# Eight more weight slices decoded by halves, two more chunks of the attention turned on VectorE, and a reordered first part of the step list

## The chip, the cores and the metric

The kernel runs on one core of a Trainium2 chip. The metric is the device time of one execution in microseconds (us); lower is better. Engines are called PE (TensorE, with PEld for its weight loads), DVE (VectorE), ACT (ScalarE), POOL (GpSimd) and SP (SyncE, which issues the transfers here).

## The reference

A gated linear attention layer feeds a two-layer block with a hard-swish.

```python
# q, k, v, alpha: (4, 8, 768, 48) float32
for t in range(S):
    state = alpha[:, :, t, :, None] * state + einsum('bhd,bhe->bhde', k[:, :, t], v[:, :, t])
    y[:, :, t] = einsum('bhd,bhde->bhe', q[:, :, t], state)
x = y.transpose(0, 2, 1, 3).reshape(3072, 384)
h = x @ w_in                       # (384, 2048), float64 as it comes in
g = h * clip(h + 3, 0, 6) / 6
out = g @ w_out                    # (2048, 384), float64 as it comes in
```

## The kernel before

**Chunks and groups.** The 3072 tokens are 24 chunks of 128, six to each of the four batches. Two chunks make a group for the two dense layers. Groups 0 and 1 run the first layer with plain matmuls (`ff1` at L493, `ff1_half` at L504); group 0 also runs the second layer so (`ff2`, L531). From then on both layers run by schemes with fewer products: the first layer in 20 products per group (`product1`, L617), the second in seven (`product`, L720).

**The step list.** Nothing is looped or scheduled by the compiler. One string of 1798 words, run by `run` under `manual_schedule`, gives the program order of every engine. A word is a step and its arguments: `la.1` loads alpha of chunk 1, `f.1.7.0` is `ff1` of group 1, pair of columns 7, into PSUM bank m0. Each engine takes its own instructions from this list strictly in order, and waits where an input is not there or a buffer is not free.

**Steps of the attention, by chunk j:** `la lk lq lv` (loads, SP), `ta tk tq` (turning alpha, k, q so that head dimensions lie on partitions), `ca` (alpha to its place), `r` and `p` (scans, L321 and L333, DVE), `k` and `q` (scaled k and q, DVE), `sc` (scores, PE L360), `m` (masked scores, DVE L370), `kb` and `ck` (k by token, PE L388 and ACT L392), `u` (state update, PE L444), `sm` (next state, DVE L454), `st` (POOL L423), `sv` and `qa` (state and q laid beside the values and scores, ACT L433 and L380), `ya` and `yb` (the two halves of the output, PE L470), `cy` (output kept as the dense layer's input, ACT L479).

**Two ways to turn a chunk.** For a chunk below `FIRST` a load is one transfer of 192 KB in rows of 192 B into `rings`; `ta`, `tk`, `tq` are four PE transposes each (L283) into a PSUM bank, and `ca` is an ACT copy (L312). From `FIRST` on a load is four transfers in rows of 640 and 768 B (352 KB in all, each row once for two bands of partitions) into `quads`, with two small POOL memsets (L259) the first time that each of the two buffers is used; `tk` and `tq` are DVE transposes by 32x32 blocks in pairs (`turned`, L291), `ca` is the DVE transpose `by_blocks` (L287), `k` and `q` read SBUF instead of PSUM (L343), and `q` is followed by a small POOL memset (L347).

**Weights.** They come as float64. The kernel loads 16 slices (`w.0` to `w.7` of `w_in`, `w.8` to `w.15` of `w_out`, 768 KB each) into five raw buffers (`HOMES` says which) and turns each into float32:

- `d1` (`round_low`, ACT L185) rounds the low word, `d2` (`magnitude`, ACT L195) takes the high word without its sign.
- `d3` (`high_bits`, DVE): for a slice in `BY_HALVES` two instructions (L202 and L204), for the others three (L206, L207 and L209; the third puts the sign back).
- `dx` (`sign`, ACT L190), only for a slice in `BY_HALVES`: one instruction that writes the sign into the upper half of the low word.
- `d4` (`add_low`, POOL L216) adds the two words and frees the raw buffer.

`w_in`'s slice i serves column pair i of the first layer (`fa.i`, `fb.i`, `f.g.i`), and two slices of `w_out` serve a quarter of `ff2` (`b.c.part`).

**Around the dense layers.** `fr` (ACT L509) and `fg` (DVE L513) gate a bank of `ff1` and so free it; there are four such banks. `x` and `y` (DVE L664 and L554 to L558) prepare the weight sums of the later schemes, `s`, `xc` and `o` (DVE) the other sums. `z.m.n` (`idle`, L548) multiplies the identity n times into bank m: filler that keeps PE running. Until step 424 there are 46 such blocks.

Of the kernel before, what the change touches and what calls it, by code (L numbers as in the profile page):

```python
# [17 lines left out]
def kernel(  # L18
# [153 lines left out]

    BY_HALVES = {0, 1, 2, 4}

    def slice_of(i):
# [2 lines left out]
        return dst, lo, hi  # L180
# [31 lines left out]
    def add_low(i):  # L212

        dst, lo, hi = slice_of(i)
        high = dst if i in BY_HALVES else hi
        nc.gpsimd.tensor_tensor(out=dst.bitcast(I32), in0=high.bitcast(I32),  # L216
# [59 lines left out]
    def transposed(name, j, i=None):  # L276
        if j >= FIRST:
            turned(name, name, j)
            return
        t = bank("t" + name, j, i)  # L280
        src = ring[name, j % NR]
        for p in range(NP):
            nc.tensor.transpose(  # L283
                t[:, p], src[:, 2 * p : 2 * p + 2].rearrange("s h d -> s (h d)"), ident)
# [5 lines left out]
    def turned(to, name, j):  # L290
        nc.vector.transpose(  # L291
            out=turns[to].rearrange("r w p (u b) -> r p w b u", b=V // 2),
            in_=quads[name, j % NQ].rearrange("r p (w b) d -> r p w b d", w=2)[..., 0:BLK])
# [42 lines left out]
    def scaled(name, j):  # L336

        t = (K_t if name == "k" else Q_t)[j] = (Ks if name == "k" else Qs)[j % 2]
        by = R_t[j][:, :, 1:W] if name == "k" else without_first(P_t.pop(j))
        if j < FIRST:  # L340
            nc.vector.tensor_tensor(out=t, in0=ps_t.pop(("t" + name, j)), in1=by, op=ALU.mult)
# [428 lines left out]

    with tc.manual_schedule():
        run("""la.1 z.0.2 z.0.5 ta.1.2 la.0 ca.1 lq.1 z.0.2 ta.0.3 z.0.2 w.0 r.1 p.1 tq.1.2 z.0.2
               la.2 z.0.2 ca.0 r.0 z.0.2 lk.0 z.0.8 q.1 d1.0 p.0 lq.0 dx.0 ta.2.0 z.0.2 lv.0.0 d2.0
               tk.0.1 z.0.2 k.0 lk.1 w.1 tq.0.2 ca.2 kb.0.1 z.0.2 w.2 q.0 ck.0 r.2 qa.0.1 lq.2
               sc.0.0.2 z.0.2 z.0.2 la.3 qa.1.0 z.0.3 qa.1.1 m.0 p.2 lk.2 u.0.1.3 tk.1.0 lv.1.1
               z.0.2 w.3 d2.1 d1.1 sm.0.0 k.1 sv.0.1 dx.1 la.4 kb.1.1 z.0.1 ck.1 sm.0.1 sv.0.0
               tq.2.3 d3.0 d1.2 sc.1.2.1 d4.0 d3.1 lk.3 st.1 z.0.3 dx.2 q.2 m.1 d2.2 z.0.2 tk.2.3
               ta.3.0 k.2 ca.3 d3.2 u.1.2.1 sv.1.0 r.3 lq.3 sm.1.0 sm.1.1 ya.0.3 yb.0 cy.0 ta.4.0
               d4.1 fa.0.1 sv.1.1 ca.4 fa.1.2 sc.2.2.1 p.3 d2.3 d4.2 d3.3 ya.1.0 yb.1 w.5 d1.3 m.2
               fa.2.0 tk.3.3 lv.3.0 d4.3 k.3 w.6 cy.1 lk.4 st.2 fb.2 kb.2.2 kb.3.1 r.4 lv.2.2 d2.5  # L780
               d1.5 fr.0.2.0 fb.1 ck.2 tq.3.0 qa.2.0 d3.5 tk.4.3 d1.6 k.4 q.3 f.0.3.3 ck.3 sv.2.0
               d2.6 sc.3.2.1 u.2.0.1 u.3.2.3 qa.3.1 fr.0.3.1 d4.5 w.7 fg.0.2 lq.4 d3.6 f.0.5.0
               sm.2.0 d2.7 w.8 fg.0.3 d1.7 sv.2.1 kb.4.0 d4.6 ck.4 sm.2.1 st.3 d2.8 la.5 d3.7 sv.3.0
               qa.3.0 sm.3.0 w.9 f.0.6.3 qa.2.1 lk.5 d4.7 sv.3.1 tq.4.0 fb.0 m.3 sm.3.1 fr.0.1.0
               ta.5.1 p.4 fg.0.1 d3.8 w.4 fr.0.5.1 ca.5 fg.0.5 fr.0.0.0 d1.8 ya.2.2 yb.2 w.10 d4.8
               cy.2 fg.0.0 lq.5 ya.3.3 yb.3 cy.3 d2.9 la.6 f.0.7.2 lv.4.1 d1.9 d3.9 f.1.7.0 d4.9 r.5
               fr.0.7.0 d1.4 fr.0.6.1 dx.4 d1.10 w.12 q.4 fg.0.7 p.5 fg.0.6 d2.4 f.1.1.1 d2.10 d3.4
               tq.5.2 fr.1.7.1 tk.5.1 fr.1.1.0 la.7 f.1.0.2 d2.12 k.5 f.1.3.3 lv.5.0 ca.6 w.11 d4.4
               fg.1.7 lk.6 fg.1.1 fr.1.3.1 d3.10 d1.12 q.5 f.1.6.0 fr.1.0.0 fg.1.3 fg.1.0 qa.0.0
               d3.12 d4.10 lk.7 qa.5.0 ca.7 f.1.2.1 d2.11 kb.5.3 st.4 fr.1.6.1 tk.6 ck.5 f.1.4.2  # L790
               w.13 qa.4.0 fg.1.6 d1.11 sc.5.1.0 sc.4.3.2 u.4.3.0 u.5.1 d4.12 fa.4.3 d3.11 d4.11 m.4
               fr.1.4.1 fr.1.2.0 f.1.5.0 fb.4 w.15 lq.6 sm.4.0 fg.1.2 b.0.0.1 fg.1.4 d2.13 d1.13
               sv.4.1 r.6 d3.13 w.14 fr.0.4.0 b.1.0.2 k.6 sm.4.1 d2.15 sv.4.0 fg.0.4 tq.6 b.0.1
               fr.1.5.1 d1.15 b.1.1 d3.15 p.6 d4.13 st.5 fg.1.5 qa.4.1 tk.7 d2.14 s.1.1.1 s.1.0.0
               d1.14 d3.14 d4.15 qa.5.1 m.5 kb.6.3 b.0.2 d4.14 P.1.0.0 sm.5.0 s.1.3.2 s.1.2.3
               P.1.1.3 y.1 q.6 lk.8 x.0 x.1 K.1.0 lk.9 y.5 y.0 y.3 sv.5.0 x.2 sv.5.1 b.0.3 s.1.5
               ck.6 b.1.2 y.2 y.6 r.7 b.1.3 lv.6.2 y.9 G.1.0.0 P.1.2 k.7 K.1.1 y.8 y.10 y.7 y.11
               la.8 s.1.4 y.4 ya.4.1 yb.4 bo.1 cy.4 xc.2.0 ya.5.0 yb.5 cy.5 xc.2.1 y.16 sc.6.3.2
               u.6.1.2 P.1.3.3 K.1.2 xc.2.3 y.12 P.1.4 xc.2.4 y.15 x.3 so.1 lv.7.0 G.1.1.1 y.13
               P.1.5 bo.0 y.17 xc.2.5 y.19 P.1.6 xc.2.7 G.1.2.2 y.20 xc.2.6 y.18 O.1.2 y.21 M.2.0.2  # L800
               y.23 M.2.15.3 n.2.0.8 xc.2.2 M.2.1 xc.2.8 n.2.1.9 la.9 M.2.16 ca.8 sm.6.0 sv.6.1
               G.1.3.3 xc.2.9 sm.6.1 tk.8 p.7 m.6 r.8 la.10 kb.7.1 M.2.2 M.2.7.0 y.14 lq.7 n.2.2.10
               M.2.3 M.2.4 lq.8 n.2.7.11 M.2.8 n.2.4.12 p.8 ck.7 z.1.3 st.7 o.2.0.0 M.2.18.1 e.2.0.0
               xc.2.10 M.2.9 sv.7.0 tq.7 O.1.3 h.2.0 o.2.1.0 M.2.5 q.7 e.2.1.1 k.8 h.2.1 tk.9 M.2.10
               kt.8 n.2.10.14 u.7.0.2 y.22 n.2.5.13 sc.7.1.2 n.2.18.10 qa.6.1 M.2.11 n.2.11.15
# [149 lines left out]
```

## Time and profile before

| | |
|---|---|
| time, median of 3 runs | 531.0 us (530.9 to 531.11) |
| the profiled execution | 530.91 us, span 529.1 us |
| PE busy | 520.6 us (98% of the span) |
| DVE busy | 462.0 us (87%) |
| ACT busy | 259.6 us (49%) |
| POOL busy | 55.3 us (10%) |
| transfers | 54.4 MB, 42.8% of 16 DMA engines' time |
| granted TensorE clock, mean | 0.999 |

Busy time is the time with at least one instruction of that engine under way, over the span from the first to the last instruction. Matmuls are pipelined, so PE's rate is better read from start to start than from the busy time of one. 1.8 us of the execution's time lie outside the span.

### The profile page before, as it was taken

Reading aid. Unit: us, or ns where it says so; the run is one execution under the profiler, and the core shown is the slowest. Engines: PE = TensorE matmul, PEld = TensorE weight load, DVE = VectorE, ACT = ScalarE, POOL = GpSimd, SP = SyncE. Lnnn points to the kernel's source line nnn. Section 1 sums busy time; section 2 is a strip of 40 time slices with the busy share of each in tenths; the row PEclk is TensorE's granted clock in tenths of the full one; section 3 lists DMA queues with packets and bytes.
Section 4 is the critical chain, followed back from the end, with each engine's and each line's share of the span. In section 5 each row is a group of like instructions: output and inputs, shape, how many; then the busy total and the mean of one; then the engine's idle time right before and its main releaser. Section 6 shows DMA issues by size and latency. Waiting matters only on the chain.

```text
span 529.1 us, 15082 instructions
## 1 busy us (share of the span) xinstructions
PE 520.6 (98%) x6290; PEld 494.8 (94%) x6290; DVE 462.0 (87%) x838; ACT 259.6 (49%) x513; POOL 55.3 (10%) x89
## 2 busy tenths in 40 slices
PE   8799999999999999999999999999999999999997
PEld 6598886789999999999999999999999999999997
DVE  6998999999999999999999999899988896395471
ACT  4968875112755453464365355454353552543330
POOL 5333543100000100101000000000000000000000
PEclk9999999999999999999999999999999999999999
DMA  9998794213245365445452546153330214000001
GB/s 180 253 240 261 181 269 117 54 32 93 58 118 118 92 135 135 104 95 150 82 145 63 110 118 160 41 124 79 108 84 25 61 22 100 17 26 7 9 9 37
DMA packets 124100, 54.40 MB, mean 103 GB/s; under 512 B 83328, under 2 KB 116864, under 8 KB 124032
## 3 DMA queue, kind: packets, MB, share of 16 engines
q1 hardware_dynamic: 124032, 53.44, 42.8%
q8 instruction: 49, 0.80, 0.7%
q14 instruction: 19, 0.16, 0.1%
HBM read 44.50 MB, written 8.91 MB: 101 GB/s over the span
## 4 chain that ended last, share of the span: by engine, by line
PE 90%; DVE 4%; SPq 2%; DMA 2%; ACT 1%; issue 1%; POOL 0%; DVEq 0%; POOLq 0%; ACTq 0%
PE m_ps L720 36%; PE m_ps L617 31%; PE m_ps L493 6%; PE m_ps L531 4%; PE t_ps L470 4%; PE t_ps L360 2%; PE m_ps L504 2%; PE m_ps L548 2%; PE t_ps L444 1%; PE t_ps L283 1%; DMA rings<-in_alpha_dram 1%; DVE g_sb L554 1%; SPq L253 1%; PE t_ps L388 1%; SPq L410 0%
## 5 line engine op out<-in xcount | busy, mean ns | idle before, releaser
L720 PE MATMUL m_ps<-w,g_sb 128*128 128x192 f32 x704 | 121.8, 327 | 0.0
L623 ACT COPY g_sb<-m_ps 128x512 f32<-128x512 f32 x110 | 63.5, 583 | 116.6 <-PE m_ps L617 91.6
L720 PEld LDWEIGHTS m_ps<-w,g_sb 128*128 128x128 f32 x704 | 113.8, 190 | 0.5
L720 PE MATMUL m_ps<-rings,g_sb 128*128 128x192 f32 x528 | 91.3, 326 | 0.0
L720 PEld LDWEIGHTS m_ps<-rings,g_sb 128*128 128x128 f32 x528 | 85.4, 190 | 0.3
L617 PE MATMUL m_ps<-xc,w 128*128 128x128 f32 x640 | 82.1, 276 | 0.3 <-ACT g_sb L623 0.3
L617 PEld LDWEIGHTS m_ps<-xc,w 128*128 128x128 f32 x640 | 77.7, 192 | 1.2 <-ACT g_sb L623 0.4
L509 ACT ACTIVATE r<-g_sb,half 128x512 f32<-128x512 f32 x80 | 56.8, 721 | 36.3 <-DVE g_sb L558 17.5
L513 DVE SCALAR_TENSOR_TENSOR g_sb<-r,g_sb 128x512 f32<-128x512 f32 x80 | 53.8, 684 | 9.1 <-ACT r L509 8.7
L617 PE MATMUL m_ps<-xT,raw 128*128 128x128 f32 x400 | 53.2, 278 | 0.0
L617 PEld LDWEIGHTS m_ps<-xT,raw 128*128 128x128 f32 x400 | 48.8, 192 | 0.7 <-ACT g_sb L623 0.2
L664 DVE TENSOR_TENSOR g_sb<-g_sb 128x512 f32<-128x512 f32 (+1 forms) x55 | 42.2, 796 | 4.8 <-PE m_ps L720 4.5
L617 PE MATMUL m_ps<-xT,w 128*128 128x128 f32 x320 | 41.8, 277 | 0.0
L617 PEld LDWEIGHTS m_ps<-xT,w 128*128 128x128 f32 x320 | 39.0, 192 | 0.4
L380 ACT COPY A<-q 48x256 f32<-48x256 f32 x88 | 35.4, 402 | 2.9 <-PE t_ps L470 0.8
L370 DVE TENSOR_TENSOR A<-t_ps,mask 64x256 f32<-64x256 f32 x96 | 36.1, 415 | 0.4
L493 PE MATMUL m_ps<-xT,w 128*128 128x256 f32 x144 | 32.5, 381 | 0.0
L617 PE MATMUL m_ps<-xc,raw 128*128 128x128 f32 x240 | 31.9, 276 | 0.0
L321 DVE TENSOR_TENSOR_SCAN R<-t,ones 128x516 f32<-128x516 f32 x24 | 29.5, 1228 | 2.7 <-ACT t L312 2.7
L423 POOL TENSOR_TENSOR st<-sm,R 128x192 f32<-128x192 f32 x20 | 14.7, 737 | 157.2 <-DVE sm L454 157.1
L554 DVE TENSOR_TENSOR g_sb<-g_sb 128x512 f32<-128x512 f32 x40 | 26.9, 679 | 4.1 <-ACT g_sb L623 4.1
L554 DVE TENSOR_TENSOR g_sb<-m_ps,g_sb 128x512 f32<-128x512 f32 x30 | 20.5, 683 | 11.4 <-PE m_ps L617 7.0
(107 smaller groups left out, 718.2 us busy)
## 6 DMA issues: line engine op xcount, KB each, us to landing
raw<-in_moe_w_out_dram SPq DMA_DIRECT2D x8, 768.0 KB, 5.6
raw<-in_moe_w_in_dram SPq DMA_DIRECT2D x6, 768.0 KB, 6.8
v<-in_v_dram SPq DMA_DIRECT2D x48, 96.0 KB, 3.2
out_dram<-oh SPq DMA_DIRECT2D x44, 96.0 KB, 1.7
far<-kq SPq DMA_DIRECT2D x64, 64.0 KB, 2.2
kb<-far SPq DMA_DIRECT2D x64, 64.0 KB, 2.0
aq<-in_alpha_dram SPq DMA_DIRECT2D x36, 96.0 KB, 2.5
kq<-in_k_dram SPq DMA_DIRECT2D x36, 96.0 KB, 2.7
```

The lines of the kernel that those rows point to most:

```text
L321: nc.vector.tensor_tensor_scan(out=reverse(R, n - 1, n), data0=reverse(ax, n, n), data1=reverse(ones, n, n), initial=0.0, op0=ALU.mult, op ...
L370: nc.vector.tensor_tensor(out=to[:, a], in0=sc[a][half], in1=mask[half, half].unsqueeze(1).to_broadcast([HB, NP, HB]), op=ALU.mult)
L380: nc.scalar.copy(out=to[:, a], in_=Q_t[j][64 * a : 64 * a + D, :, half])
L470: nc.tensor.matmul(y_of(j, (i + 1) // 2, p)[:, HB * b : HB * b + HB], vb[:, p, e : e + 32], A_t[j][:, b, 2 * p + a], start=(b == 0 and i = ...
L493: nc.tensor.matmul(h[:, f], w1[:, kk, o : o + C], xT_t[g][:, kk], start=(kk == 0), stop=(kk == KT - 1))
L509: nc.scalar.activation(out=to, in_=h, func=AF.Relu, bias=half, scale=1.0 / 6.0)
L513: nc.vector.scalar_tensor_tensor(out=to, in0=r, scalar=1.0, in1=h, op0=ALU.min, op1=ALU.mult)
L554: eng.tensor_tensor(out=out, in0=in0, in1=in1, op=ALU.add if s1 > 0 else ALU.subtract)
L617: nc.tensor.matmul(acc[g][i][:, f * C : (f + 1) * C], spots[w][:, f * C : (f + 1) * C], x_of(g, x), start=(first and f == 0), stop=last, s ...
L623: nc.scalar.copy(out=slots[z], in_=acc[g][i])
L664: nc.vector.tensor_tensor(out=out, in0=in0, in1=in1, op=ALU.subtract)
L720: nc.tensor.matmul(to[g], a, rhs[:, f], start=(first and f == 0), stop=(last and f == HF - 1), skip_group_check=True)
```

## The change

`BY_HALVES` grows from slices 0, 1, 2 and 4 to slices 0 to 3 and 8 to 15: slice 4 now goes the long way, and slices 3 and 8 to 15 by halves. `FIRST` goes from 6 to 4: chunks 4 and 5 are loaded in blocks and turned on DVE. The first 424 words of the step list are replaced by 430 others; the other 1374 words stay. Leaving out PSUM bank numbers, the new part holds the same steps as the old one, except that `ta.4`, `ta.5` and `dx.4` are gone and `dx.3` and `dx.8` to `dx.15` are new. The fillers are again 46 blocks.

```diff
-    BY_HALVES = {0, 1, 2, 4}
+    BY_HALVES = {0, 1, 2, 3, 8, 9, 10, 11, 12, 13, 14, 15}
...
-    FIRST = 6
+    FIRST = 4
...
-        run("""la.1 z.0.2 z.0.5 ta.1.2 la.0 ca.1 lq.1 z.0.2 ta.0.3 z.0.2 w.0 r.1 p.1 tq.1.2 z.0.2
-               la.2 z.0.2 ca.0 r.0 z.0.2 lk.0 z.0.8 q.1 d1.0 p.0 lq.0 dx.0 ta.2.0 z.0.2 lv.0.0 d2.0
-               tk.0.1 z.0.2 k.0 lk.1 w.1 tq.0.2 ca.2 kb.0.1 z.0.2 w.2 q.0 ck.0 r.2 qa.0.1 lq.2
-               sc.0.0.2 z.0.2 z.0.2 la.3 qa.1.0 z.0.3 qa.1.1 m.0 p.2 lk.2 u.0.1.3 tk.1.0 lv.1.1
-               z.0.2 w.3 d2.1 d1.1 sm.0.0 k.1 sv.0.1 dx.1 la.4 kb.1.1 z.0.1 ck.1 sm.0.1 sv.0.0
-               tq.2.3 d3.0 d1.2 sc.1.2.1 d4.0 d3.1 lk.3 st.1 z.0.3 dx.2 q.2 m.1 d2.2 z.0.2 tk.2.3
-               ta.3.0 k.2 ca.3 d3.2 u.1.2.1 sv.1.0 r.3 lq.3 sm.1.0 sm.1.1 ya.0.3 yb.0 cy.0 ta.4.0
-               d4.1 fa.0.1 sv.1.1 ca.4 fa.1.2 sc.2.2.1 p.3 d2.3 d4.2 d3.3 ya.1.0 yb.1 w.5 d1.3 m.2
...
+        run("""z.0.2 z.0.2 z.0.2 w.1 la.0 z.0.2 la.1 z.0.3 lk.0 d2.1 ta.0.0 z.0.3 ca.0 lq.0 w.0
+               z.0.2 z.0.5 tk.0.2 z.0.2 la.2 d3.1 tq.0.1 d1.1 dx.1 ta.1.3 r.0 p.0 d4.1 k.0 kb.0.2
+               z.0.1 z.0.8 z.0.2 z.0.2 w.2 q.0 ca.1 d1.0 lq.1 ck.0 r.1 la.3 d2.0 qa.0.1 lk.1 ta.2.2
+               p.1 tq.1.0 z.0.2 ca.2 r.2 d1.2 lv.0.0 d2.2 q.1 z.0.2 ta.3.0 z.0.2 sv.0.0 tk.1.3 d3.2
+               w.3 u.0.1.2 sc.0.1.2 dx.0 d3.0 dx.2 k.1 sm.0.0 d4.2 m.0 d1.3 sv.0.1 qa.1.1 d4.0 z.0.2
+               lq.2 sm.0.1 st.1 lv.1.1 ya.0.3 yb.0 kb.1.1 p.2 cy.0 ck.1 lk.3 tq.2.2 q.2 ca.3 w.7
+               z.0.2 qa.1.0 d2.3 r.3 lk.2 sc.1.1.3 u.1.1.0 sm.1.0 sm.1.1 w.5 fa.0.1 sv.1.0 m.1 d3.3
+               dx.3 fa.1.2 sv.1.1 tk.3.0 st.2 d4.3 k.3 tk.2.3 qa.2.1 qa.2.0 lq.3 ya.1.2 yb.1 cy.1
+               d2.5 w.6 fa.2.0 lk.4 k.2 lv.2.2 d2.7 fb.2 tq.3.1 p.3 d1.5 d1.7 d3.5 q.3 f.0.3.3
+               sv.2.0 fr.0.2.0 d2.6 fg.0.2 kb.2.1 fb.1 lv.3.0 qa.3.0 ck.2 kb.3.3 d3.7 fr.0.3.1 ck.3
+               d4.5 d3.6 fb.0 w.8 u.2.3.2 sm.2.0 sm.2.1 d1.6 d4.6 fg.0.3 f.0.5.0 u.3.1.0 sc.2.2.3
+               la.4 fr.0.1.0 fg.0.1 sc.3.1.0 tk.4 qa.3.1 w.9 ca.4 st.3 la.5 sv.2.1 d1.8 f.0.6.3 d2.8
+               d3.8 dx.8 w.4 sm.3.0 fr.0.5.1 d4.7 sv.3.0 m.3 m.2 r.4 k.4 sv.3.1 lq.4 f.0.7.2 ya.2.1
+               yb.2 d4.8 fg.0.5 w.11 lk.5 ya.3.3 d1.9 dx.9 d2.9 d3.9 yb.3 d4.9 ca.5 cy.2 cy.3
+               fr.0.0.0 w.12 fr.0.6.1 fg.0.0 d2.4 sm.3.1 lq.5 p.4 kb.4.2 fg.0.6 f.1.7.0 fr.0.7.0
...
```

More of the change, by code (lines that the diff above doesn't have):

```diff
@@ L771 @@
     with tc.manual_schedule():
-        run("""la.1 z.0.2 z.0.5 ta.1.2 la.0 ca.1 lq.1 z.0.2 ta.0.3 z.0.2 w.0 r.1 p.1 tq.1.2 z.0.2
-               la.2 z.0.2 ca.0 r.0 z.0.2 lk.0 z.0.8 q.1 d1.0 p.0 lq.0 dx.0 ta.2.0 z.0.2 lv.0.0 d2.0
-               tk.0.1 z.0.2 k.0 lk.1 w.1 tq.0.2 ca.2 kb.0.1 z.0.2 w.2 q.0 ck.0 r.2 qa.0.1 lq.2
-               sc.0.0.2 z.0.2 z.0.2 la.3 qa.1.0 z.0.3 qa.1.1 m.0 p.2 lk.2 u.0.1.3 tk.1.0 lv.1.1
-               z.0.2 w.3 d2.1 d1.1 sm.0.0 k.1 sv.0.1 dx.1 la.4 kb.1.1 z.0.1 ck.1 sm.0.1 sv.0.0
-               tq.2.3 d3.0 d1.2 sc.1.2.1 d4.0 d3.1 lk.3 st.1 z.0.3 dx.2 q.2 m.1 d2.2 z.0.2 tk.2.3
-               ta.3.0 k.2 ca.3 d3.2 u.1.2.1 sv.1.0 r.3 lq.3 sm.1.0 sm.1.1 ya.0.3 yb.0 cy.0 ta.4.0
-               d4.1 fa.0.1 sv.1.1 ca.4 fa.1.2 sc.2.2.1 p.3 d2.3 d4.2 d3.3 ya.1.0 yb.1 w.5 d1.3 m.2
[L780 to L802, printed above, removed]
@@ new lines @@
+        run("""z.0.2 z.0.2 z.0.2 w.1 la.0 z.0.2 la.1 z.0.3 lk.0 d2.1 ta.0.0 z.0.3 ca.0 lq.0 w.0
[13 more added lines that the diff above has]
+               fr.0.0.0 w.12 fr.0.6.1 fg.0.0 d2.4 sm.3.1 lq.5 p.4 kb.4.2 fg.0.6 f.1.7.0 fr.0.7.0
+               fr.1.7.1 fg.0.7 d1.4 f.1.1.1 d1.11 tq.4 q.4 d3.4 f.1.0.2 st.4 fg.1.7 tk.5 fr.1.1.0
+               fg.1.1 dx.11 d2.11 la.6 r.5 d1.12 fr.1.0.0 d4.4 f.1.3.3 k.5 d3.11 dx.12 fr.1.3.1 p.5
+               f.1.6.0 fg.1.3 ck.4 d2.12 d3.12 d4.12 w.10 d1.10 fr.1.6.1 kb.5.0 f.1.2.1 fg.1.0 lk.6
+               lv.4.1 w.15 ca.6 tq.5 ck.5 fa.4.3 lv.5.0 fr.1.2.0 fb.4 sv.4.0 fg.1.2 qa.0.0 f.1.4.2
+               fg.1.6 d4.11 d2.10 r.6 b.0.0.1 lq.6 qa.4.0 u.5.3 u.4.0.2 sc.4.0.1 tk.6 dx.10 fr.1.4.1
+               fr.0.4.0 q.5 sc.5.3.2 qa.4.1 d3.10 p.6 f.1.5.0 qa.5.1 d4.10 fg.1.4 d1.15 fg.0.4 d2.15
+               dx.15 sm.4.0 w.14 d1.14 b.0.1 fr.1.5.1 d3.15 lv.6.2 sv.4.1 k.6 w.13 b.1.0.2 m.5
+               fg.1.5 d2.14 d4.15 qa.5.0 sm.4.1 st.5 tq.6 d2.13 y.3 dx.14 d1.13 sv.5.0 lk.7 d3.14
+               d3.13 s.1.0.0 sm.5.0 la.8 b.1.1 sv.5.1 m.4 P.1.0.0 la.7 y.5 kb.6.1 q.6 d4.14 dx.13
+               ya.5.3 yb.5 ya.4.2 yb.4 d4.13 y.1 tk.7 ca.8 ca.7 cy.5 x.0 sc.6.0.3 s.1.1.1 y.0 ck.6
+               u.6.0.1 b.1.2 P.1.1.3 b.1.3 cy.4 xc.2.1 xc.2.3 x.1 x.2 bo.1 y.6 s.1.3.2 y.9 y.10
+               K.1.0 s.1.2.3 y.7 b.0.2 G.1.0.0 la.9 y.11 y.2 P.1.2 xc.2.4 K.1.1 s.1.4 P.1.3.3 y.8
+               P.1.4 so.1 s.1.5 y.4 y.12 y.16 K.1.2 y.15 xc.2.5 P.1.5 y.13 y.17 b.0.3 y.19 y.18 y.21
+               lk.9 y.20 xc.2.0 M.2.0.2 xc.2.6 bo.0 G.1.1.1 r.7 k.7 G.1.2.2 n.2.0.8 lk.8 kb.7.2
+               M.2.15.3 xc.2.8 lv.7.0 xc.2.7 M.2.16 y.23 M.2.1 O.1.2 x.3 P.1.6 xc.2.2 n.2.1.9 sm.6.0
+               sv.6.1 G.1.3.3 xc.2.9 sm.6.1 tk.8 p.7 m.6 r.8 la.10 M.2.2 M.2.7.0 y.14 lq.7 n.2.2.10
```

## The prediction

> **What bounds the kernel now.** I read the page's busy shares first, then busy time by stretch, then what PE waited for, then instructions in order of time.
>
> Busy time by stretch; columns are stretch, length, busy us of each engine, granted clock, DMA share, GB/s:
>
> ```profile
> 24.00:28.37 4.37, 3.24 (x108) 2.68 (x107) 4.26 (x9) 2.79 (x6) 2.15 (x2) 1.00 1.28 264
> 28.37:55.70 27.33, 27.33 (x474) 25.02 (x472) 25.14 (x42) 22.48 (x42) 9.16 (x8) 1.00 0.98 261
> 55.70:95.00 39.30, 39.30 (x288) 31.43 (x287) 38.55 (x62) 26.59 (x41) 18.21 (x21) 1.00 0.73 177
> 95.00:125.00 30.00, 30.00 (x333) 26.05 (x332) 28.43 (x46) 4.56 (x12) 0.68 (x4) 1.00 0.13 34
> ```
>
> From 28.37 us (`fa.0`) PE is never idle: what is saved on PE there is saved at the end, if nobody else becomes late. But DVE has only 2.2 us free of 27.3 up to 55.7 and 0.75 of 39.3 after, and ACT 4.85 of 27.3. Before 28.37 PE waits (us in all, times, longest):
>
> ```profile
> PE t_ps L283 <- DMA rings<-in_q_dram: 1.5, 1, 1.5
> ...
> PE t_ps L388 <- DVE k L341: 1.0, 1, 1.0
> ```
>
> The groups that the change touches (us in all, mean ns of one):
>
> ```profile
> L287 DVE STREAM_TRANSPOSE t<-aq 128x512 f32<-128x512 f32 x18 | 19.8, 1110 | 0.3 <-POOL t L347 0.3
> ...
> L291 DVE STREAM_TRANSPOSE kt<-kq 128x512 f32<-128x512 f32 x18 | 12.7, 704 | 0.0
> ...
> L283 PE MATMUL t_ps<-ident,rings 128*128 128x128 f32 x72 | 11.0, 284 | 2.3 <-DMA rings<-in_q_dram 1.5 <-DMA rings<-in_alpha_dram 0.8
> ...
> L209 DVE SCALAR_TENSOR_TENSOR raw<-raw,w 128x768 uint32<-128x768 uint32 x11 | 10.8, 978 | 0.4
> ...
> L190 ACT ACTIVATE raw<-raw 128x768 f16<-128x768 int32 x3 | 5.8, 1938 | 0.1
> ```
>
> Means hold some overlap with the next instruction; I count from start to start. In order of time:
>
> ```profile
> 58.32 0.73 ACT L509 ACTIVATE r<-m_ps,half 128x512 f32<-128x512 f32 x1
> 58.88 2.00 ACT L190 ACTIVATE g_sb<-g_sb 128x768 f16<-128x768 int32 x1
> 60.55 1.06 ACT L185 ACTIVATE raw<-raw 128x768 int32<-128x768 uint32 x1
> ...
> 61.00 1.04 PE L283 MATMUL t_ps<-ident,rings 128*128 128x128 f32 x8
> 61.87 0.38 PE L493 MATMUL m_ps<-xT,w 128*128 128x256 f32 x1
> ```
>
> A sign (L190) holds ACT 1.67 us (58.88 to 60.55), a PE transpose costs 0.87/8 = 0.109 us.
>
> **The engine totals.**
> PE: 6 steps of 4 transposes go (`ta tk tq` of chunks 4, 5): 24 x 0.109 = -2.6 us. Fillers: 46 blocks in both orders. Nothing else of PE's changes.
> DVE: 9 slices lose L209 and slice 4 gains it: -8 x 0.88 (start to start) = -7.0. Chunks 4 and 5 gain one L287 (0.95) and two L291 (0.63) each: +4.4. `k` and `q` cost the same from SBUF as from PSUM (L343 0.68, L341 0.68). Net -2.6, as much as PE saves, so DVE is no closer to the bound than now.
> ACT: +8 x 1.67 signs, less two `ca` copies (L312, 0.58): +12.2.
> POOL: 16 adds as before; the memsets of the first two `quads` uses move from chunks 6 and 7 to 4 and 5; two L347 memsets of 0.1 are new.
> SP and queue: six transfers (0.5 us of SP each) become 24 (0.47 each): +8.3 us of SP. By the packets' starts in the trace a load in 192 B rows takes 1.1 us of the queue, one in 640/768 B rows 1.9 us, a weight slice 2.5 us, and data are usable some 0.9 us after the last packet. So six loads cost +5 us of queue, mostly between 35 and 62 us, where its share is 0.98.
>
> **The start.** Loads run one after another from 1.5 us. In the new order `w.3` has three slices and nine small loads ahead of it: 1.5 + 4 x 2.5 + 9 x 1.12 = 21.6, usable at 22.5. ACT comes to `d1.3` before that and waits; behind it stand `sv.0.1` (23.9 done), then PE's `yb.0` (24.5), ACT's `qa.1.1`, `cy.0`, `ck.1`, `ca.3` (26.3; it frees the bank of `u.1`), `u.1`, and `fa.0` starts at 26.8. PE has done 17.7 us of work by then, so 9.1 us are lost; before it was 28.37 with 18.6 done, 9.8 lost. Waits for `lq.1` (PE idle from 14.4 to 16.6) and `lv.0` lie inside this.
>
> **Up to group 1** (`f.1.7`, at 55.7 before). ACT is the close one. Three more signs (3, 8, 9) stand before it, less two `ca`: 5.0 - 1.1 = +3.9 us, against 4.85 us of ACT idle there. Going down ACT's order from `fa.0`, waiting where an input is later, I get `cy.1` 32.8, `fr.0.2` 37.2, `ck.3` 40.2, `dx.8` 46.2, then `d1.9`, which waits for `w.9`: it is queued on SP behind the raw buffer that `d4.6` frees (POOL, about 44.6) and usable at 48.6. So `dx.9` 51.1, `cy.3` 53.3. DVE: `d3.6` 42.2, `ca.4` 45.5, `m.2` 49.8, needed by PE at 50.5. PE itself, with 43.5 us of work before `f.1.7` (45.3 before: 1.8 less), would be there at 53.1. So `f.1.7` starts at 53.3 if nothing collides.
>
> **Collisions** are in the trace of before, and I add them by the rows:
>
> ```profile
> 20.70 1.86 POOL L216 TENSOR_TENSOR w<-w,raw 128x768 int32<-128x768 int32 x1 [13.14 <-DVE w L204]
> 20.96 0.68 ACT L392 COPY kb<-t_ps 128x512 f32<-128x512 f32 x1
> 21.09 2.03 DVE L204 TENSOR_SCALAR w<-w 128x768 uint32<-128x768 uint32 x1
> ```
>
> L204 took 2.03 us beside 0.69 at 19.77, since the add was running. Others: the scan L333 at 29.16 1.90 for 1.23, L206 at 44.84 1.11 for 0.55: 1.2 us between 28 and 56. Bounds here: 0 (all hidden in DVE's waits) to 2.7 (two of L204's 1.34); I take 0.8, between nothing and what the same stretch shows now. `f.1.7` then starts at 54.1. The Trainium skill ("SBUF — State Buffer", "Who interferes with whom") calls it an exclusive lock: the later of a two-port VectorE instruction and a GpSimd one waits the other out whole. By that rule one full block by an add of 1.47 us, in place of my 0.8, would give 529.2 us; the trace agrees in the rows above.
>
> **After `f.1.7`.** PE's work from there to the end was 529.1 - 55.7 = 473.4; of the 2.6 us saved 1.8 lie ahead, so 472.6 remain. ACT gets the signs 10 to 15 and loses that of slice 4, +8.4 us by `P.1.1` (about 97 us), where it now has 12.7 us free in 55.7 to 95: in order it comes to the end of `dx.13` at about 91, and the add ends some 4 us early. DVE is 0.5 us better off towards PE than now. I put no new wait here; if that cover goes, the late one is `d4.13` for `P.1.1`.
>
> Sum: 54.1 + 472.6 + 1.8 outside the span = 528.5 us, 2.4 below the profiled 530.91 (median 531.0).
>
> **Rivals.**
> 1. *ACT comes too late (slower).* For it: ACT runs without a break from 50 to 60 us now (9.90 of 10), and free time in pieces can't all be used. Place: `cy.2`/`cy.3` behind `d1.9 dx.9 d2.9`. If only half of the +3.9 finds room, `f.1.7` starts at 55.7 + 1.95 = 57.65: 57.65 + 472.6 + 1.8 = 532.1; if none does, 534.0. It decides from `f.1.7` at 56.5 on (530.9). Against: my chain has ACT 0.2 us from PE there, not 3. Chance 0.18.
> 2. *Late fetches (no change).* `w.9`, `la.5`, `w.4`, `lq.4` stand behind one wait on SP for `d4.6`, behind a longer queue. If `w.9` is usable 3 us later (one block load of 1.9 us and 1.1 of POOL ahead), `cy.3` ends at 56.3, `f.1.7` at 56.5: 530.9. For: the queue is full there (0.98). Chance 0.13.
> 3. *The clock falls.* PE idles 2.2 us in one piece and is half idle up to 24 us. In the trace the clock stayed at 1.00 through gaps of 1.5 us. At the start fillers took 0.85 us for two blocks instead of 0.43 up to about 5.9 us; the same for 4.4 us after 16.6 would double 3.6 us of PE work, of which the wait for `w.3` hides about 2.1: `f.1.7` +1.5, 530.0 us. Chance 0.06. The Trainium skill ("TensorE: Matmul & The Clock Gate", "What's actually happening") gives half rate after an idle window of about 3.4 us; no gap of mine is that long.
> 4. *DVE holds the suffix.* It is 99% busy from 130 to 200 us (39.60 of 40 from 160 to 200). If collisions eat its -2.6 us, PE's saving is waited away: 531.1. Chance 0.04.
> 5. *The change doesn't do it:* if the freed PE time only becomes idle time at the start (`fa.0` at 28.4 or later), 530.1 or more. Chance 0.03.
>
> **How the numbers follow.** Forecast 0.56. A difference under 0.2% (1.06 us) can't be told from none here, so faster means below 529.9, slower above 532.1. Faster: 0.56 + some of 3 = 0.59. Slower: rival 1's upper part and tails of 2 and 4 = 0.24. The rest, 0.17, is no change. Range: low end 527.3 (no collision, 527.7, and 0.4 for the start's arithmetic); high end 532.8 (rival 1 with 0.65 of its 3.9 on the path: 58.2 + 472.6 + 1.8 = 532.6).
>
> **What would show it.** L283 x48, L209 x4, L190 x12, L287 and L291 x20. `fa.0` near 26.8 and `f.1.7` near 54 in the order of time; ACT over 90% busy from 28 to 54; no PE idle after. It is wrong if ACT's `cy.3` starts over 2 us after `yb.3`, if PE waits at `ya.2`, `b` or `P.1.1`, or if `w.3` or `w.9` come over 2 us later than said.

## The result: slower, 536.5 us, and the profile after

| | before | after |
|---|---|---|
| time, median | 531.0 us (530.9 to 531.14, 6 runs) | 536.52 us (535.18 to 538.97, 6 runs) |
| ratio | | 1.0106, 95% interval 1.0093 to 1.0119 |
| the profiled execution | 530.91 us, span 529.1 | 535.18 us, span 533.4 |
| PE, DVE, ACT, POOL busy | 520.6, 462.0, 259.6, 55.3 us | 519.0, 462.3, 272.9, 57.1 us |

The instruction counts came as the change says. The groups after (us in all, mean ns of one, idle time before):

```profile
L287 DVE STREAM_TRANSPOSE t<-aq 128x512 f32<-128x512 f32 x20 | 21.9, 1110 | 0.3 <-POOL t L347 0.3
...
L190 ACT ACTIVATE raw<-raw 128x768 f16<-128x768 int32 x11 | 21.1, 1947 | 0.1
...
L291 DVE STREAM_TRANSPOSE kt<-kq 128x512 f32<-128x512 f32 x20 | 14.1, 706 | 0.0
...
L283 PE MATMUL t_ps<-ident,rings 128*128 128x128 f32 x48 | 7.1, 277 | 2.4 <-DMA rings<-in_q_dram 1.4 <-DMA rings<-in_alpha_dram 0.9
```

Busy time by stretch, cut at `fa.0` (27.51) and `f.1.7` (56.16). Columns: stretch, length, then busy us of PE, PEld, DVE, ACT, POOL, granted clock, DMA share, GB/s:

```profile
24.00:27.51 3.51, 3.45 (x106) 2.73 (x107) 3.41 (x4) 3.40 (x9) 2.52 (x2) 1.00 1.14 274
27.51:56.16 28.65, 27.30 (x467) 24.42 (x465) 26.82 (x46) 27.28 (x44) 11.29 (x17) 1.00 0.90 228
56.16:95.00 38.84, 38.84 (x284) 31.40 (x285) 36.68 (x62) 34.23 (x49) 13.34 (x12) 1.00 0.82 204
95.00:125.00 30.00, 26.48 (x308) 21.98 (x308) 27.75 (x41) 4.58 (x9) 3.76 (x3) 1.00 0.20 51
```

PE, without a wait from 28.37 to 125 before, now loses 1.35 us before `f.1.7` and 3.5 us between 95 and 125. DVE stands 2.2 us in 56 to 95, where it stood 0.75. What PE waited for (us in all, times, longest):

```profile
PE m_ps L720 <- DVE g_sb L664: 3.5, 1, 3.5
...
PE t_ps L283 <- DMA rings<-in_q_dram: 1.4, 1, 1.4
PE t_ps L470 <- issue: 1.0, 1, 1.0
```

So there are two new waits. The first row is `P.1.2` at 112.72. The third is a stop in the middle of `yb.1`, to which the profile gives no releaser ("issue"); in order of time:

```profile
31.26 0.75 PE L470 MATMUL t_ps<-A,v 128*32 128x64 f32 x36
32.99 0.64 PE L470 MATMUL t_ps<-A,v 128*32 128x64 f32 x28 [0.98 <-issue]
```

The wait of `P.1.2` can be followed through three engines in order of time. ACT:

```profile
90.15 0.91 ACT L195 ACTIVATE w<-raw 128x768 f32<-128x768 f32 x1 [1.31 <-DMA raw<-in_moe_w_out_dram]
```

DVE, with what it waits for and the sum that `P.1.2` needs:

```profile
91.09 0.56 DVE L202 TENSOR_SCALAR w<-w 128x768 f32<-128x768 f32 x1 [1.36 <-ACT w L195]
...
97.93 2.33 DVE L554 TENSOR_TENSOR raw<-w 128x512 f32<-128x512 f32 x1 [2.05 <-POOL w L216]
...
111.89 0.69 DVE L664 TENSOR_TENSOR g_sb<-g_sb 128x512 f32<-128x512 f32 x1
```

POOL, the memset and the two adds `d4.14` and `d4.13`:

```profile
95.94 0.11 POOL L347 MEMSET t<- 128x4 f32 x1 [7.82 <-DVE q L343]
96.03 3.67 POOL L216 TENSOR_TENSOR w<-w,raw 128x768 int32<-128x768 int32 x2
```

`w.13` lands late, so `d2.13` on ACT and `d3.13` on DVE stand 1.3 us. Then `y.1` (97.93) needs the raw buffer that `d4.14` frees. That add's sign `dx.14` ended near 92.7, but the add stood on POOL behind the little memset of `q.6`, which waits for DVE's own `q.6`. DVE waits 2.05 us for POOL, and `y.1` then takes 2.33 us beside the second add, against 0.68 for the same shape at 104.89. DVE makes up none of it, and its `s.1.2` (111.89) is what PE waits for.

### The profile page after: what moved, and what is told of

Same layout as the page of the kernel before. It is cut to its first block, busy times and chain, and to the rows that moved or that the text cites. A ratio compares the mean times of both kernels' runs of the same rounds, so it can differ in the third digit from the quotient of the medians.

```text
span 533.4 us, 15070 instructions
## 1 busy us (share of the span) xinstructions
PE 519.0 (97%) x6266; PEld 492.0 (92%) x6266; DVE 462.3 (87%) x836; ACT 272.9 (51%) x519; POOL 57.1 (11%) x91
## 4 chain that ended last, share of the span: by engine, by line
PE 71%; DVE 14%; DMA 4%; ACT 4%; issue 4%; SPq 2%; POOL 1%; DVEq 0%; POOLq 0%; ACTq 0%
PE m_ps L720 32%; PE m_ps L617 31%; PE t_ps L470 3%; PE t_ps L360 2%; DMA raw<-in_moe_w_out_dram 1%; PE t_ps L444 1%; DVE g_sb L513 1%; DMA g_sb<-in_moe_w_in_dram 1%; DVE g_sb L554 1%; DVE R L321 1%; DMA raw<-in_moe_w_in_dram 1%; DVE A L370 1%; DMA v<-in_v_dram 1%; DVE t L287 1%; ACT raw L190 1%
## 5 line engine op out<-in xcount | busy, mean ns | idle before, releaser
L617 PEld LDWEIGHTS m_ps<-xT,w 128*128 128x128 f32 x320 | 39.0, 192 | 0.4
L617 PE MATMUL m_ps<-xc,raw 128*128 128x128 f32 x240 | 31.9, 276 | 0.0
L493 PEld LDWEIGHTS m_ps<-xT,w 128*128 128x128 f32 x144 | 26.6, 190 | 4.2 <-issue 0.4
```

The costliest lines, as they stand in the source:

```text
L493: nc.tensor.matmul(h[:, f], w1[:, kk, o : o + C], xT_t[g][:, kk], start=(kk == 0), stop=(kk == KT - 1))
L617: nc.tensor.matmul(acc[g][i][:, f * C : (f + 1) * C], spots[w][:, f * C : (f + 1) * C], x_of(g, x), start=(first and f == 0), stop=last, s ...
```

## The experiments

Times are medians. In each table row or text the ratio is to the kernel before on the same chip. The step list is the text of the diffs; `...` leaves words out.

### 1. One word on POOL, and two trials of single parts

e_pool puts `d4.14` ahead of `q.6`:

```diff
- ... y.5 kb.6.1 q.6 d4.14 dx.13 ...
+ ... y.5 kb.6.1 d4.14 q.6 dx.13 ...
```

> The changed kernel with one word moved: d4.14 (the add of slice 14 on POOL) stands before q.6 instead of behind it, so that it no longer waits behind the small memset that follows q.6 on POOL. Theory (one queue position): in the changed kernel DVE's y.1 waited 2.05 us for this add and then took 2.33 us instead of 0.69 beside the next add; both go, so PE's wait of 3.5 us for the sums before P.1.2 goes almost whole: a profile of about 531.7 us against 535.2, the median 3 to 3.5 us under the changed kernel's. Rival (DVE is late for other reasons, the added load of ACT and the late fetch of w.13): PE's wait at P.1.2 stays over 2.5 us and the time moves by less than 1 us.

Measured: 532.59 us (531.91 to 537.49), ratio 1.0034 (1.0014 to 1.0054), profiled 532.14. That is 3.9 us less than after, 3.0 in the profiled executions. The add runs at 93.33, ahead of the memset (POOL of e_pool):

```profile
93.33 1.85 POOL L216 TENSOR_TENSOR w<-w,raw 128x768 int32<-128x768 int32 x1 [4.59 <-ACT raw L190]
96.39 0.10 POOL L347 MEMSET t<- 128x4 f32 x1 [1.21 <-DVE q L343]
```

PE of e_pool passes `P.1.2` (109.83) without a wait:

```profile
104.67 5.32 PE L531 MATMUL m_ps<-w,g_sb 128*128 128x384 f32 x16
109.83 2.76 PE L720 MATMUL m_ps<-rings,g_sb 128*128 128x192 f32 x16
```

So one place in POOL's queue held more than half of the loss. This kernel is the base of most of what follows.

p_halves makes only the first part of the change in the kernel before, p_first4 only the second:

```diff
- BY_HALVES = {0, 1, 2, 4}
+ BY_HALVES = {0, 1, 2, 3, 8, 9, 10, 11, 12, 13, 14, 15}
  # and each dx.i right behind d1.i in the list of before, dx.4 taken out
```

> The kernel before with the decoding by halves alone: BY_HALVES as changed, each new sign step directly behind its d1, no dx.4; order and FIRST as before. DVE has 7.0 us less, ACT 13.4 us more. Theory (ACT has room only in pieces): PE waits for ACT's copies between 45 and 100 us, 532 to 536 us. Rival (ACT's idle time takes it in, and DVE's gain serves nobody since PE is the bound): 530.5 to 531.5 us.

```diff
- FIRST = 6
+ FIRST = 4
  # and ta.4, ta.5 taken out of the list of before; tk, tq of 4 and 5 without a bank
```

> The kernel before with FIRST = 4 alone: chunks 4 and 5 turned by DVE, ta.4 and ta.5 gone, the rest of the order as before. PE has 2.6 us less, DVE 4.4 us more, the queue 5 us more. Theory (PE's saving reaches the end as long as DVE's lateness is hidden): 528.5 to 530 us. Rival (DVE is full from 28 us on and hands its 4.4 us to PE, and the block loads come late): 531.5 to 535 us, with waits of PE for DVE between 45 and 125 us.

Measured: 534.54 us, ratio 1.0056 (1.0036 to 1.0077), and 540.08 us, ratio 1.016 (1.014 to 1.018). What PE waited for in p_halves:

```profile
PE m_ps L493 <- DVE g_sb L513: 1.9, 1, 1.9
...
PE m_ps L493 <- ACT xT L479: 1.1, 1, 1.1
```

And in p_first4:

```profile
PE t_ps L470 <- issue: 3.2, 2, 2.9
PE t_ps L360 <- DVE q L341: 1.7, 1, 1.7
```

Put into the old order, the signs make ACT late: PE waits 1.1 us for `cy`, and 1.9 us for a `fg` of DVE, which had itself stood 1.63 us for ACT's `d2` (L195) at 65.98. So ACT's free time can't all be used there. The turned chunks make DVE's in-order queue late (1.7), and there is an "issue" wait of 2.9 us that I could not explain then. A part of p_first4's 9 us is the clock: in its profile it is at half rate from 45.0 to 48.4 and from 58.7 to 62.1, and all four executions have a mean of 0.990 to 0.993. Each part alone, in the old order, is slower; both together in the old order were not run.

### 2. What made `f.1.7` late: not ACT, not the collisions

In e_pool `f.1.7` starts at 56.94, with a stop of 1.8 us in `yb.1`. My first theory was that the new sign `dx.3` on ACT keeps `yb.1`'s values waiting (e_dx3; v1 moves three more things of ACT's).

```diff
- ... d3.3 dx.3 fa.1.2 sv.1.1 tk.3.0 ...                 # e_dx3 and v1
+ ... d3.3 fa.1.2 sv.1.1 dx.3 tk.3.0 ...
- ... m.0 d1.3 sv.0.1 ... q.2 ca.3 ... p.3 d1.5 d1.7 d3.5 q.3 f.0.3.3 sv.2.0 fr.0.2.0 ...   # v1
+ ... m.0 sv.0.1 ... q.2 ca.3 d1.3 ... p.3 sv.2.0 fr.0.2.0 d1.5 d1.7 d3.5 q.3 f.0.3.3 ...
```

> Base: the changed kernel with d4.14 ahead of q.6 (532.59 us, f.1.7 at 56.94 in its profile). Here dx.3 also goes behind sv.1.1 on ScalarE. Theory A (ScalarE's new sign stands before the v copies that PE's yb.1 waits for): the 1.8 us of PE idle at 31.9 goes, yb.1's second half starts near 32.1, f.1.7 near 55.2, 530.8 us. Rival B (the collisions of POOL's adds with VectorE set f.1.7, so time won at yb.1 is waited away later): f.1.7 stays at 56.5 to 57, 532.2 to 532.6 us.

> As the kernel with dx.3 moved, and sv.2.0 and fr.0.2 go ahead of d1.5 and d1.7 and d1.3 behind ca.3, all on ScalarE. Theory A: ScalarE's order alone made the start late, so f.1.7 comes near 54.5, as I had forecast for the change itself, and the time is 530.0 us, below both kernels. Rival B (collisions, or VectorE's order): no better than the kernel with dx.3 moved alone, 530.8 to 532.6 us.

Measured: e_dx3 531.74 us, ratio 1.0011 (1.0 to 1.0023), `f.1.7` at 55.51 and no stop. v1 532.36 us, ratio 1.0024 (1.0014 to 1.0034), with a stop of 1.25 us. The first looked like theory A; the second, which has the same move, did not. Two more kernels make the signs, or the adds, almost free:

```diff
+        if i in {3, 8, 9}:                             # e_signs, in sign
+            halves, hi = halves[:, :, 0:2], hi[:, :, 0:2]
+        if i in {0, 1, 2, 3, 5, 6, 7, 8, 9}:           # e_adds, in add_low
+            dst, lo, high = dst[:, :, 0:2], lo[:, :, 0:2], high[:, :, 0:2]
```

> Base as before; the signs of slices 3, 8 and 9 write 6 of 768 columns only, so these slices' signs are left out, with every wait in its place: ScalarE is spared 3 x 1.5 us before f.1.7. Theory A: PE's idle time at yb.1 goes and f.1.7 comes near 54.5, 530.1 us. Rival B: the collisions remain, f.1.7 at 56 or later, 531.7 us or more.

> Base as before (d4.14 ahead of q.6); POOL's adds of slices 0 to 3 and 5 to 9 work on 6 of 768 columns only, so their low bits are left out, with every wait in its place. Theory A (ScalarE sets the start; VectorE's lost time lies in its waits): the scans and tensor_scalars beside the adds fall back to 1.2 and 0.7 us, some 3.5 us of VectorE in all, yet yb.1 keeps its wait and f.1.7 gains under 1 us: 531.6 to 532.6 us. Rival B (collisions set it): f.1.7 near 54, 529.7 us.

Measured: e_signs 532.34 us, ratio 1.0024 (1.0011 to 1.0036); e_adds 533.1 us, ratio 1.0035 (1.0018 to 1.0051). `f.1.7` came at 56.74 and 56.49. PE in `yb.1` of e_signs:

```profile
31.41 0.75 PE L475 MATMUL t_ps<-A,v 128*32 128x64 f32 x36
33.62 0.58 PE L475 MATMUL t_ps<-A,v 128*32 128x64 f32 x26 [1.47 <-issue]
```

ACT ahead of it, the shortened sign and the copy of the values:

```profile
29.25 0.22 ACT L195 ACTIVATE g_sb<-g_sb 128x6 f16<-128x6 int32 x1
29.36 0.71 ACT L438 COPY v<-s 48x192 f32<-48x192 f32 x2
```

ACT had the values ready at 30.1, and PE still stood until 33.62, after the same 36 matmuls. In e_adds DVE is busy 2.1 us less in the first 56 than in e_pool (45.96 against 48.02; the scan at 24 us takes 1.22 instead of 2.31), and `f.1.7` gained 0.45, of which 0.36 is a shorter stop. Both theories fall: e_signs speaks against the signs, e_adds against the collisions. By these two profiles the collisions cost some 0.1 us at `f.1.7`, since DVE gives the time back by waiting less. The median of e_adds says less than its profile: five of its ten executions have a mean clock of 0.997, the other five take 530.74 to 532.54 us.

### 3. PE waits for its own code

The page's third part lists, beside the data, packets that carry instructions (queue and kind: packets, MB, share):

```profile
q1 hardware_dynamic: 121248, 54.43, 43.3%
q8 instruction: 49, 0.80, 0.6%
```

These are 49 packets of 16 KB, and 49 x 256 = 12544 is about PE's 12622 recorded instructions (6266 matmuls, as many weight loads, 87 waits and 3 drains). Counting all of these in order in each trace, every stop in `yb.1` comes right behind number 705, and a smaller one (up to 1.0 us, in e_fill, just before `fa.0`) behind number 449 = 705 - 256; the 2.9 us of p_first4 come behind number 1473 = 705 + 3 x 256. The packets' own records give their start:

| kernel | packet starts | PE comes to 705 | goes on | from the packet's start |
|---|---|---|---|---|
| before | 27.85 | 31.8 | no stop | (3.9) |
| after | 30.38 | 31.8 | 32.99 | 2.6 |
| e_pool | 31.34 | 31.9 | 33.85 | 2.5 |
| e_signs | 31.12 | 31.9 | 33.62 | 2.5 |
| e_adds | 30.95 | 32.1 | 33.73 | 2.8 |
| v1 | 30.45 | 31.8 | 33.27 | 2.8 |
| e_dx3 | 29.66 | 31.9 | no stop | (2.3) |

PE never went on sooner than 2.3 us behind the packet's start. The same holds beyond this table. If the first packet belongs to number 449, the second to 705 and so on in steps of 256, the 20 traces have 964 such borders, and PE passed none of them sooner than 2.2 us behind its packet's start; the 22 waits of over 0.5 us at a border all ended 2.4 to 3.1 us behind it. When PE calls for a packet isn't recorded. Counted from when PE passes number 449 (26.0 before, 26.3 after, 26.1 in e_pool), the packet started 1.9 us later in the kernel before, 4.1 after, 5.3 in e_pool. From one border to the next PE needs some 5.6 us here and the packet 2.6, so by this count a lag well over 3 us is a stop (e_dx3, with 3.5, just passes).

To test this, 32 or 64 short matmuls in PE's wait for `lq.1` move every border to an earlier step:

```diff
+            nc.tensor.matmul(bank_m[m][0:32, 0:64], ident[:, 0:32], ident[:, 0:64], start=True, stop=True)
- ... p.1 tq.1.0 ...
+ ... p.1 c.0.32 tq.1.0 ...      # e_code64; c.0.64 in e_code128
- ... lk.8 kb.7.2 M.2.15.3 xc.2.8 lv.7.0 xc.2.7 M.2.16 ...      # only v2 (on v1), v2b (on e_dx3), with c.0.32
+ ... lk.8 M.2.15.3 xc.2.8 lv.7.0 xc.2.7 M.2.16 kb.7.2 ...
```

> Base: d4.14 ahead of q.6 (532.59 us; in its profile PE stands from 32.1 to 33.85 in the middle of yb.1). Neither spared signs nor spared adds took that stall away. Theory C: PE waits there for its own code. PE's instructions come in 16 KB packets of the DMA queue, 256 at a time, and in five runs with the stall PE went on 2.5 to 2.8 us after the start of such a packet, always at the same instruction of the recorded order (the 705th). Here 32 short matmuls (64 instructions; in the wait for lq.1, at no cost) shift every block border 64 instructions to the left, to the start of yb.1, and the call for the packet to before the slow matmuls of fa.0. Theory C: the packet starts near 27.5 and not at 31.3, no stall in yb.1, f.1.7 near 55.2, 530.9 us. Rival D (the stall belongs to what yb.1 reads, v or A): it stays in yb.1's second half, 532.6 us.

> The same with 64 short matmuls (128 instructions). Theory C: the border now lies at the first matmuls of fa.0, about 1 us behind the call, so PE stands there instead: a stall of 1 to 2.5 us near 27.8 in fa.0, none in yb.1, 532.5 to 533.5 us. Rival D: the stall stays in yb.1's second half, 532.6 us.

> The kernel with dx.3, sv.2.0, fr.0.2 and d1.3 moved on ScalarE (532.36 us; stalled 1.25 us at yb.1, f.1.7 at 56.41), with 64 instructions of short matmuls, and with kb.7 behind M.2.16 on PE (there PE waits 0.5 us for VectorE's k.7 near 123). Theory C: f.1.7 near 55.1, 0.5 less behind it, 530.5 us, below the kernel before. Rival D: 531.9 us.

> The kernel with only dx.3 moved (531.74 us; no stall at yb.1 in its profile, f.1.7 at 55.51), with the same short matmuls and kb.7. Theory C: nothing to gain at yb.1 in its profile, some in executions in which the packet came late; 0.5 us at kb.7: 531.1 us. Rival D: 531.2 us, the same.

Measured: 535.38 (ratio 1.0075, 1.0059 to 1.0092), 537.73 (1.0121, 1.0105 to 1.0137), 536.87 (1.0107, 1.0088 to 1.0127), 535.44 us (1.0075, 1.0055 to 1.0096). All four are slower, by an error of mine: in e_code64's PE row below, each short matmul is recorded as two, each with a weight load, so 32 of them are 128 instructions and take 3.76 us, 2.3 more than the wait that they were to fill.

```profile
15.54 3.76 PE L547 MATMUL m_ps<-ident 128*32 128x64 f32 x64
```

PE of v2 in `fa.0`:

```profile
29.92 0.82 PE L504 MATMUL m_ps<-xT,w 128*128 128x128 f32 x5
32.02 2.39 PE L504 MATMUL m_ps<-xT,w 128*128 128x128 f32 x19 [1.28 <-issue]
```

As times they are useless, as a test they are not. The shift is 128, which puts number 705 into `fa.0`, as I had expected of a shift of 128. v2 has its stop there, after five matmuls of `fa.0`, 2.76 us behind its packet (29.26), and `yb.1` runs through. In e_code64 the packet is as early (29.17), `fa.0` starts only at 31.54, and there is no stop. v2b, with the same shift, waits 0.34 us in `fa.0`, 2.8 us behind its packet (29.55). In e_code128 the shift is 256, so no border lies in `fa.0` and the stop that I expected there did not come; number 961 now lies in `yb.1`, its packet (34.83) has started 2.9 us before PE gets there, and PE does not stop. So the stop moves with the border and hangs on its packet; what `yb.1` reads has nothing to do with it. e_code64's 128 more instructions also bring a 50th packet.

Last, data ahead of the packet. e_queue brings a third of the bytes of two slices; v7 and v7b move `w.7` behind `w.5`; v8 and v8b move `w.5` behind the loads of chunk 4; e_kb7 is e_dx3 with `kb.7` moved.

```diff
-            nc.sync.dma_start(out=to, in_=moe_w_in[:, ...])          # e_queue, slices 5 and 7
+            nc.sync.dma_start(out=to[:, 0:1], in_=moe_w_in[0:C, ...])
- ... ca.3 w.7 ... sm.1.1 w.5 fa.0.1 ...                             # v7 (on v1), v7b (on e_dx3)
+ ... ca.3 ... sm.1.1 w.5 w.7 fa.0.1 ...
- ... sm.1.1 w.5 fa.0.1 ... cy.1 d2.5 w.6 fa.2.0 lk.4 k.2 ...        # v8 (on e_dx3), v8b (on v1)
+ ... sm.1.1 fa.0.1 ... cy.1 lk.4 w.5 d2.5 w.6 fa.2.0 k.2 ...
- ... lk.8 kb.7.2 M.2.15.3 xc.2.8 lv.7.0 xc.2.7 M.2.16 ...           # v7, v7b, e_kb7
+ ... lk.8 M.2.15.3 xc.2.8 lv.7.0 xc.2.7 M.2.16 kb.7.2 ...
```

> Base: d4.14 ahead of q.6 (532.59 us; stall of 1.8 us at yb.1, code packet started at 31.34). The loads of the weight slices 5 and 7 bring one third of their bytes (two of three row blocks are left out, so these slices hold old data); every instruction and wait stays. Two loads of 2.5 us become 0.8 us ahead of the code packet. Theory C (the packet stands in the queue behind data): it starts some 3 us earlier, near 28, the stall at yb.1 goes, f.1.7 near 55.2, 530.9 us. Rival D (PE calls for it late): the packet starts at 30 to 31.3 as before, the stall stays, 532.6 us.

> The kernel with dx.3, sv.2.0, fr.0.2 and d1.3 moved on ScalarE (532.36 us; stall 1.25 us), with w.7 behind w.5 on SyncE, which leaves a hole in the queue near 24 us, and kb.7 behind M.2.16 on PE. Theory C: the code packet starts near 28 to 29, no stall, f.1.7 near 55.1, 0.5 us less at kb.7: 530.5 us. Rival D: 531.9 us.

> The kernel with only dx.3 moved (531.74 us), with w.7 behind w.5 and kb.7 behind M.2.16. Theory C: no stall at yb.1, in every execution: 531.0 us. Rival D: 531.2 us. If w.6 or the block loads behind w.7 come too late for ScalarE, f.0.6 waits: 533 us.

> The kernel with only dx.3 moved (531.74 us), with kb.7 behind M.2.16 on PE. If VectorE's k.7 is late for kb.7 alone, the 0.5 us of PE idle near 122.5 go: 531.2 us. If VectorE as a whole sets the pace behind group 1, the next product waits instead: 531.7 us.

> The kernel with only dx.3 moved (531.74 us; its code packet started at 29.66 in the profiled execution), with the block loads of lk.4 and then w.5 behind lq.3 on SyncE, so that a slice of 2.5 us goes from ahead of the code packet to behind it. Theory C: the packet starts at 29.5 or earlier, stall at yb.1 under 0.5 us, 531.2 us. If SyncE or the queue are only shifted: the packet at 30 to 31.5, 532 us or more, and w.5 late for d1.5 on ScalarE as well.

> The same move in the kernel with dx.3, sv.2.0, fr.0.2 and d1.3 moved (532.36 us, stall 1.25 us). Theory C: the packet at 29.5 or earlier, 531.0 us. Else 532.4 us or more.

| kernel | time | ratio | packet starts | stop at 705 |
|---|---|---|---|---|
| e_queue | 531.24 us | 1.0003 (0.9994 to 1.0011) | 29.86 | 0.5 us |
| e_kb7 | 532.6 | 1.0027 (1.0018 to 1.0037) | 31.25 | 1.7 |
| v7 | 533.45 | 1.005 (1.0034 to 1.0067) | 31.64 | 2.4 |
| v7b | 533.28 | 1.0051 (1.0032 to 1.0071) | 30.64 | 1.3 |
| v8 | 534.32 | 1.007 (1.005 to 1.0091) | 29.17 | 0.3 |
| v8b | 533.93 | 1.0052 (1.004 to 1.0065) | 29.36 | 0.3 |

The column of stops is the time between two matmuls' starts. e_queue against e_pool, the same order with fewer bytes: the packet starts 1.5 us earlier (I had said 3), the stop falls from 2.0 to 0.5, `f.1.7` comes at 55.48 instead of 56.94, and the time falls by 1.35 us. e_dx3 and e_kb7, though, have one order up to 100 us, and their profiled packets are 1.6 us apart: the packet's place is partly chance, and that e_dx3 has no stop is not shown to come from its moved sign. So one pair of profiles can't prove that the packet stands behind data. What speaks for it is the fall of the median, and the profiles of all kernels of the new order whose number 705 lies in `yb.1`: with both slices ahead of the packet it starts at 30.3 to 31.6 us in nine of ten, with fewer bytes there (e_queue, v8, v8b) at 29.2 to 29.9 in all three. `w.7` behind `w.5` opened no hole (packet at 30.6 and 31.6). `w.5` behind chunk 4's loads did bring the packet forward, and both stops nearly go, but the slice is now late for ACT, and `q.3`, behind that slice's `d3.5` on DVE, for PE. ACT of v8:

```profile
36.63 1.72 ACT L195 ACTIVATE w<-raw 128x768 f32<-128x768 f32 x2 [2.73 <-DMA raw<-in_moe_w_in_dram]
```

PE of v8:

```profile
40.64 0.66 PE L388 MATMUL t_ps<-ident,k 128*128 128x128 f32 x4 [2.01 <-DVE q L341]
```

e_kb7 answers a smaller question: the wait of 0.5 us for `k.7` near 123 us moved to the next product (PE of e_kb7, second row; 0.5 us from start to start), so PE waits for DVE there in either order.

```profile
122.94 1.05 PE L617 MATMUL m_ps<-xc,raw 128*128 128x128 f32 x8
124.34 1.83 PE L617 MATMUL m_ps<-xT,raw 128*128 128x128 f32 x14 [0.35 <-DVE oh L740]
```

No kernel that computes everything beats the one before; e_dx3 comes to 1.0011 of it.

### 4. The clock

After's runs lie up to 3.8 us apart, with mean granted clocks of 0.993 to 1.0; e_fill was to test whether filler in the early gaps ends that.

```diff
- ... ta.2.2 p.1 ... sc.0.1.2 dx.0 ... ya.0.3 yb.0 ...
+ ... ta.2.2 z.0.4 z.0.4 p.1 ... sc.0.1.2 z.0.4 dx.0 ... ya.0.3 z.0.2 yb.0 ...
```

> The changed kernel with 14 more filler blocks (z) in the places where PE waits between 15 and 24 us: 8 behind ta.2, 4 behind sc.0, 2 behind ya.0. Theory (the granted clock falls in some executions because PE idles at the start): the executions of the changed kernel were 535.2 to 539.0 us with mean granted clocks of 1.000 to 0.993; with the gaps filled all clocks are 0.999 or more, the times lie within 1 us of each other and the median is 535.2 to 536. Rival (the spread comes from elsewhere, the transfers say): spread and clocks stay as they were, or the fillers themselves add 0.5 to 1.5 us.

Measured: 536.11 us, ratio 1.0091 (1.0071 to 1.0111), against 1.0106 after, with intervals that overlap; clocks from 0.993 to 1.0 again. The gap of 3.6 us at `P.1.2` was still there, and one of 0.6 in `yb.1`, so this settles only that the early gaps it filled are not the cause.

## Why the prediction was wrong, step by step

I forecast 528.5 us by 54.1 + 472.6 + 1.8. The profiled execution has 56.16 + 477.24 + 1.8 = 535.2, and the median lies 1.3 us above it. The 8.0 us split so:

- **The start** held: `w.3` usable at 22.5 (22.7), `sv.0.1` done at 23.9 (24.3), `ca.3` at 26.3 (26.5). `fa.0` came 0.7 late (27.51 for 26.8), part of it the small code wait at number 449.
- **Up to group 1** failed by 1.2 us in `yb.1`. My list of what PE could wait for had ACT, DVE and the loads; PE's own code packets, which take the same 16 DMA engines as the loads that I had counted 5 us longer, were not in it. Another 0.6 was a mis-sized term: I counted 26.7 us of PE work between `fa.0` and `f.1.7` before, where the profile had 27.33 at full busy time, and 0.4 is two short waits for DVE, at `kb.4` (0.21) and `f.1.7` (0.15). The term held a slip besides: 43.5 us of work and 9.1 lost make 52.6, not the 53.1 that I wrote.
- **Collisions** were mis-sized the other way. Up to 56 us they took more of DVE (2.1 us in e_adds) than my 0.8, but of `f.1.7` only 0.1. Blocking was real, as in the row of `y.1`; it cost the end only where DVE was last. The Trainium skill's lock ("SBUF — State Buffer", "Who interferes with whom") agrees with that row: 2.33 us less 0.68 is 1.65, and the add beside it had 1.8 us to run.
- In sum `f.1.7`: 0.7 + 1.2 + 0.6 + 0.4 - 0.8 = 2.1 late.
- **After `f.1.7`**, "I put no new wait here" was the largest error: 3.5 us at `P.1.2`. I named `d4.13` for `P.1.1` as the late one. ACT ended its sign `dx.13` at 97.1, not at 91, but still in time for that add (97.9); I had followed ACT and the add, not POOL's queue ahead of the add `d4.14`, where `q.6`'s memset waits for DVE. e_pool shows that the word `q.6` ahead of `d4.14` was the whole of these 3.5 us. Of the other 1.1 us, 0.33 is PE's wait for DVE at `kb.7`, and most of the rest is the 0.8 us that I had PE save behind `f.1.7`: less its waits PE takes 472.8 us from there to the end before (473.4 less 0.6) and 472.7 after (477.24 less 4.5). Before, too, PE was not "never idle" to the end: it waits 0.36 us at 183 and 0.25 at 276.
- **The engine totals** came out for ACT (+13.3 us for +12.2), in part for PE (520.6 to 519.0, -1.6 for -2.6), and not for DVE (462.0 to 462.3 for -2.6, collisions included). They were no use where I put them: a saving on DVE that is spent on waiting for POOL, ACT and raw buffers doesn't reach PE.

The rivals: rival 1 (ACT) was wrong in its place, since spared signs changed nothing in this order, though p_halves shows its mechanism in the old one. Rival 2's late fetch did happen, not at `w.9` but with `w.13` (1.3 us) and with code. Rival 4's end, PE waiting for DVE, came about by waits and not by collisions. Rival 3, with 0.06, came true in part: the median lies 1.3 us above the profiled execution, and of after's six runs four have a mean clock of 0.997 or less. The gap of 3.5 us at `P.1.2`, which I had not foreseen, may bring the falls: in e_pool, without it, two of twelve runs have such a clock and the median is 0.45 above the profile. It is not shown, for the profiled executions of after and e_fill pass that gap (3.52 and 3.62 us) at full clock. The range's high end, 532.8, was 0.2 above its own sum of 532.6.

## What to carry to other kernels

Follow a moved step through every in-order queue that its release passes, the one with the idle engine and the tiny memset too: a place there is worth more than the microseconds that an engine saves. Where loads are brought forward into a full queue, ask what else uses the DMA engines; PE's code does, one packet per 256 instructions, and a stretch of many short matmuls runs through its block soonest. And when a wait reads "issue", count instructions before looking for a late operand: stops at the same number in different kernels point to code.
